# Pooled attention and a routed expert layer on one core: the order of VectorE's routing operations, a tile for softmax factors, one start-up multiplication and the last rows

## The chip, the core and the metric

The kernel runs on one core of one Trainium2 chip. A core has TensorE (PE; its weight loads are a row of their own, PEld), VectorE (DVE), ScalarE (ACT), GpSimd (POOL) and SyncE (SP), which issues transfers here. The engines run their own instruction streams in order and wait for one another by semaphores. The metric is device time of one execution in microseconds (us); lower is better.

## The reference, cut to what matters

All arrays are float32: q, k, v are 8 batches x 8 heads x 576 positions x 64. Keys and values are averaged over 8 neighbouring positions (72 pooled keys). The attention output, reordered to 4608 tokens x 512, goes to a layer of 8 experts, of which each token uses the one with the largest logit.

```python
k_p = k.reshape(B, H, 72, 8, D).mean(axis=3)
v_p = v.reshape(B, H, 72, 8, D).mean(axis=3)
scores = (q @ k_p.T) / sqrt(D)
scores = scores - scores.max(-1)
attn = exp(scores); attn = attn / (attn.sum(-1) + 1e-9)
x = attn @ v_p                      # to 4608 tokens x 512
logits = x @ w_gate + modality_bias[modality_id]
e_idx = argmax(logits, axis=1)
probs = softmax(logits)             # with + 1e-9 in the sum
gate_w = probs[arange(N), e_idx]
for e in range(8):
    mask = e_idx == e
    h = maximum(x[mask] @ w1[e], 0)         # 512 x 1024
    out[mask] = gate_w[mask, None] * (h @ w2[e])   # 1024 x 512
```

## The kernel before

The attention phase (about the first 185 us) works through 36 tiles of 128 query positions in 20 steps. Two batches make five steps: two of two tiles, one *mixed* step with a single tile made of the last 64 positions of both batches, and two more of two tiles. A loop over n pipelines the steps in software: in one pass it transposes the probabilities of step n-1, multiplies them with the values, and makes the scores of steps n+1 and n+2.

Of each half step w the scores (`s_pe`, TensorE, L548 in mixed steps, L554 in others) go to `s_dve`: VectorE takes row maxima `mx` (L561) and subtracts them to `sb` (L564); `s_act` takes the exponentials `pe` (L576, L577). `t_pe` transposes them (`pp`, L583; the tail by `t4_pe`, L595) and ScalarE copies them to `pt` (L588, L602). `a_pe` multiplies `pt` with the value operand `vw` (L618, L622) into `av`. The value operand holds for each head 64 pooled values, 8 columns of values already multiplied by the gate matrix, so that logits come out of the same product, and one column of ones, so that the softmax sum does too. `v_operand` (L388 to L400) builds it out of pooled values `vp` with two masks `m_a`, `m_b` that keep one of two heads; `v_gate` (L411 to L418) computes the gate columns with TensorE in a corner of a score bank, `spare[1]`, and ScalarE copies them out (L414, L415, L417).

`x_dve` then turns `av` into the output: `s8`, the eight sums (L641, `r`), their reciprocals (L643), the logits of the eight heads `lg` (L645), and the output row times the factor, `xb` (L651, two instructions). A *late* tile, the second tile of a step from the third group on, is not divided here: ScalarE copies the raw output `xo` (L648) and the eight factors stand in extra columns of `xb`, where the expert phase applies them; their reciprocal is written there directly. `xb` goes to the table `xs` in memory (L658, L661).

Routing works on groups of nine tiles (two batches). `route(g)` returns a list of small operations: the sum over heads (L700), the addition of the bias (L701), the maximum (L702), the subtraction and ScalarE's exponential `ex` (L705, L706), the choice of expert (L709 to L711), the sum of exponentials (L728 to L730), the gate value and its four stores to `xs` (L733, L736, L738), counts (L741) and the ranks within an expert. They don't run at once: they go on a list `drip`, and `gap(n)`, called between VectorE's other operations, issues the next n of it. `gap` is called in `s_dve` between maxima and subtraction, in `x_dve` behind the sums, behind the reciprocal and at its end, and twice in the loop. So the program's order on each engine is written out by these calls. Group 0 begins to drip in step 6, group 1 in step 11, group 2 in step 16; the last group's list is run behind the loop.

GpSimd meanwhile averages keys and values (L303 to L305), builds `bias_all` (L473 to L478), and adds some masks.

The expert phase (about 185 to 617 us) handles slots of 256 rows that one expert gets: rows are gathered and transposed, `hidden(f)` makes one of eight 128-wide blocks of the hidden layer (L170, with ScalarE and VectorE splitting the result into `hx` parts, L172, L174), `second(f)` multiplies it with w2 (L1186). Each runs as three matmul groups of split operands. `evac` scales a slot's rows by the gate value (L1162). The last slot ends in `end` or, when at most 128 rows of it are in use, in `end_half`, as in the run profiled here: blocks `hidden(f)` and `second(f - 1)` alternate, then `last_rows` scales the rows, one half by VectorE (L1261) and one by ScalarE (L1262), and a scatter (L1329) writes them.

## Time and profile before

| What | us |
|---|---|
| Three runs | 621.42, 624.14, 624.22 |
| Median of the three | 624.14 |
| The profiled execution | 624.82 |
| Its span, first to last instruction | 623.1 |
| TensorE busy | 604.3 (97%) |
| VectorE busy | 420.0 (67%) |
| ScalarE busy | 347.5 (56%) |
| GpSimd busy | 258.8 (42%) |
| Mean granted clock of TensorE | 0.996 of full |

Busy times are averages over a phase of attention, in which all engines hand work to one another, and a phase of experts, in which TensorE is never idle. A place in the attention phase is therefore read from the timeline: a line there gives the start, the duration, the engine, the kernel's line, the operation, the tiles written and read, and in square brackets how long the engine had been idle before and whose work ended that. The granted clock says at which share of 2.4 GHz TensorE was let run: 0.50 is its lower level, 1.2 GHz. A time ahead of the bracket is the instruction's own, so an instruction that is held while it runs shows as a longer duration and not as idle time.

### The profile page before, as it was taken

The numbers are of one execution on the slowest core, as the hardware profiler recorded it, in microseconds if no ns is written. First come the engines' busy times: TensorE is split into PE (matmuls) and PEld (weight loads), VectorE is DVE, ScalarE is ACT, GpSimd is POOL, SyncE is SP. The second block draws the span as 40 slices with busy tenths as digits, with TensorE's granted clock in tenths as the row PEclk, the third lists the DMA queues.
The fourth block names the chain that finished last, engine by engine and source line by source line (L and its number), as shares of the span: only waits on it lengthen the run. The fifth ranks groups of instructions, "written<-read, shape, count | busy, mean of one in ns | idle before, by whom it ended". The sixth has DMA issues, their size and how long they took to land.

```text
span 623.1 us, 12548 instructions
## 1 busy us (share of the span) xinstructions
PE 604.3 (97%) x4281; PEld 548.5 (88%) x4281; DVE 420.0 (67%) x803; ACT 347.5 (56%) x657; POOL 258.8 (42%) x326
## 2 busy tenths in 40 slices
PE   6899999999999999999999999999999999999996
PEld 5789889888898998999999999999999999999995
DVE  5857798789958578566666666666666665665661
ACT  3666576788541455555555555555555555555551
POOL 7789968663000451432532532522523522522510
PEclk9999899999999999999999999999999999999999
DMA  9999979874213710210210362210215510210200
GB/s 257 301 293 325 353 201 372 259 245 137 58 45 87 263 53 35 70 36 34 70 36 35 129 210 70 69 36 35 69 36 173 192 44 22 70 37 35 69 32 25
DMA packets 61178, 76.59 MB, mean 123 GB/s; under 512 B 15407, under 2 KB 39983, under 8 KB 61104
## 3 DMA queue, kind: packets, MB, share of 16 engines
q1 hardware_dynamic: 55104, 55.98, 28.9%
q0 software_dynamic: 6000, 19.72, 9.7%
q8 instruction: 36, 0.59, 0.4%
q14 instruction: 38, 0.31, 0.2%
HBM read 119.40 MB, written 19.45 MB: 223 GB/s over the span
## 4 chain that ended last, share of the span: by engine, by line
PE 79%; DVE 5%; issue 4%; POOL 4%; DMA 3%; ACT 2%; SPq 1%; POOLq 0%; ACTq 0%; DVEq 0%
PE op L1186 31%; PE hp L170 30%; PE av L618 4%; PE xt L161 2%; PE sc L554 2%; PE av L622 2%; DMA v<-in_v_dram 1%; PE pp L583 1%; PE ph L170 1%; PE pq L529 1%; DMA out_dram<-ob,sidx 1%; POOL v L303 1%; DVE sb L564 1%; DVE hl L139 1%; DVE mx L561 1%
## 5 line engine op out<-in xcount | busy, mean ns | idle before, releaser
L136 ACT CAST hl<-raw 128x1024 fp32r<-128x1024 f32 x138 | 144.8, 1049 | 138.6 <-PE op L1186 136.6
L170 PE MATMUL hp<-xh,hl 128*128 128x256 f32 x1152 | 186.1, 284 | 0.0
L139 DVE TENSOR_TENSOR hl<-raw,hl 128x1024 fp32r<-128x1024 f32 x144 | 183.7, 1277 | 0.0
L170 PEld LDWEIGHTS hp<-xh,hl 128*128 128x128 f32 x1152 | 166.1, 189 | 10.5
L1186 PE MATMUL op<-hl,hh 128*128 128x512 f32 x554 | 173.5, 394 | 0.0
L143 POOL DMA_INDIRECT xg<-xs,gidx x38 | 55.7, 1465 | 222.9 <-DVE ob L1162 158.0
L174 DVE SCALAR_TENSOR_TENSOR hlo<-hp,hh 128x256 fp32r<-128x256 f32 x139 | 58.8, 423 | 127.4 <-ACT hh L172 127.4
L1186 PE MATMUL op<-hl,hlo 128*128 128x512 f32 x277 | 108.4, 391 | 0.0
L1186 PEld LDWEIGHTS op<-hl,hh 128*128 128x128 f32 x554 | 94.8, 189 | 12.1
L170 PE MATMUL hp<-xl,hl 128*128 128x256 f32 x576 | 92.0, 282 | 0.0
L172 ACT ACTIVATE hh<-hp 128x256 fp32r<-128x256 f32 x139 | 53.4, 384 | 49.2 <-PE hp L170 44.9
L1168 POOL DMA_INDIRECT out_dram<-ob,sidx x36 | 52.3, 1453 | 66.6 <-DMA out_dram<-ob,sidx 37.0
L170 PEld LDWEIGHTS hp<-xl,hl 128*128 128x128 f32 x576 | 79.0, 190 | 0.0
L1186 PEld LDWEIGHTS op<-hl,hlo 128*128 128x128 f32 x277 | 52.0, 188 | 11.8
L618 PE MATMUL av<-vw,pt 128*128 128x146 f32 (+1 forms) x320 | 50.8, 298 | 2.2 <-ACT pt L588 1.1
L152 POOL TENSOR_TENSOR xg<-xg 128x512 f32<-128x512 f32 x34 | 41.1, 1212 | 25.1 <-DMA xg<-xs,gidx 25.0
L618 PEld LDWEIGHTS av<-vw,pt 128*128 128x128 f32 (+1 forms) x320 | 40.7, 183 | 4.7 <-ACT pt L588 2.2
L554 PE MATMUL sc<-kt,qt 128*128 128x144 f32 x256 | 37.3, 289 | 0.6 <-ACT qt L535 0.5
L164 DVE TENSOR_TENSOR xl<-xt,xh 128x512 fp32r<-128x512 f32 x38 | 24.5, 685 | 15.6 <-ACT xh L163 15.6
L554 PEld LDWEIGHTS sc<-kt,qt 128*128 128x128 f32 x256 | 33.2, 190 | 1.5 <-ACT qt L535 0.9
L561 DVE TENSOR_REDUCE mx<-sc 128x8 f32<-128x576 f32 (+1 forms) x40 | 27.7, 692 | 9.3 <-PE sc L554 7.2
L622 PE MATMUL av<-vw,pt 128*128 128x146 f32 (+1 forms) x160 | 31.4, 295 | 0.7 <-POOL vw L418 0.4
(236 smaller groups left out, 721.2 us busy)
## 6 DMA issues: line engine op xcount, KB each, us to landing
raw<-in_moe_w_dram SPq DMA_DIRECT2D x304, 256.0 KB
xs<-xb SPq DMA_DIRECT2D x16, 528.0 KB
k<-in_k_dram SPq DMA_DIRECT2D x7, 1024.0 KB
v<-in_v_dram SPq DMA_DIRECT2D x7, 1024.0 KB
q<-in_q_dram SPq DMA_DIRECT2D x7, 1024.0 KB
v<-in_v_dram SPq DMA_DIRECT2D x16, 128.0 KB
xs<-xb SPq DMA_DIRECT2D x8, 132.0 KB
k<-in_k_dram SPq DMA_DIRECT2D x4, 256.0 KB
```

Source lines behind the costliest of these rows:

```text
L136: nc.scalar.copy(hl[f][:, 0, :], raw[f])
L139: eng.tensor_sub(hl[f][:, 1, :], raw[f], hl[f][:, 0, :].bitcast(F32))
L143: nc.gpsimd.indirect_dma_start(out=xgs[(2 * s + tt) % len(xgs)], out_offset=None, in_=xs[0:rows, :], in_offset=IndirectOffsetOnAxis(idx[:, ...
L152: nc.gpsimd.tensor_tensor(xv, xv, x[:, RX:RX + H].rearrange("p (h o) -> p h o", o=1).to_broadcast([P, H, HD]), op=ALU.mult)
L170: nc.tensor.matmul(ph, hl[f][:, w, d * P:(d + 1) * P], x[:, d, :], start=(n == 0 and d == 0), stop=(n == 2 and d == ND - 1))
L172: nc.scalar.activation(hh, ph, AF.Relu)
L174: nc.vector.scalar_tensor_tensor(hlo, ph, 0.0, hh.bitcast(F32), op0=ALU.max, op1=ALU.subtract)
L554: nc.tensor.matmul(dst, qt[:, i, :], kt[b % NB][:, :, h * SPL:(h + 1) * SPL], start=True, stop=True)
L618: nc.tensor.matmul(av[hs, u, 2 * VC * gg:2 * VC * (gg + 1)], pt[:, c, hs], vw[y][:, c].rearrange("p a x -> p (a x)"), start=(gg == 0), sto ...
L622: nc.tensor.matmul(dst4[hs], pt4[:, hs], v4[y][:, 2 * u:2 * u + 2, :], start=False, stop=True)
L1168: nc.gpsimd.indirect_dma_start(out=out[:, :], out_offset=IndirectOffsetOnAxis(idx.bitcast(U32), 0), in_=ob, in_offset=None, bounds_check=N ...
L1186: nc.tensor.matmul(o[tt], l[:, ts_], hl[f][:, w, D:2 * D], start=(f == 0 and n == 0), stop=(f == NF - 1 and n == 2))
```

## The change

Five edits:

- `gap` gets an argument `long`. The first two operations of each group's list, the sum over heads and the bias addition, are kept in a set `long_ops` and are issued only by calls with `long` set: those at the end of `x_dve`, the two behind it in the loop and the one that empties the list after the loop.
- `s_dve` no longer calls `gap` in mixed steps.
- The reciprocals go to a tile `ri` of their own (four buffers). For late tiles ScalarE copies the eight of them into the columns of `xb`.
- For batch 0 the second masked copy of the values (`m_b`) is made by VectorE in place of ScalarE.
- In `end_half` the last `hidden` block stands right behind the one before it, and the last three `second` products follow. `last_rows` is one VectorE operation.

```diff
             nc.scalar.activation(dw[:, :, 0, 0:HD], vp, AF.Copy, scale=m_a)
-            nc.scalar.activation(dw[:, :, 1, 0:HD], vp, AF.Copy, scale=m_b)
+            if b:
+                nc.scalar.activation(dw[:, :, 1, 0:HD], vp, AF.Copy, scale=m_b)
+            else:
+                nc.vector.tensor_scalar_mul(dw[:, :, 1, 0:HD], vp, m_b)
...
-        def gap(n=2):
+        long_ops = set()
+
+        def gap(n=2, long=False):
             for _ in range(n):
-                if drip and drip[0] not in held:
+                if drip and drip[0] not in held and (long or drip[0] not in long_ops):
                     drip.pop(0)()
...
             nc.vector.reduce_max(mx, scv, axis=AX.X)
-            gap()
+            if jj is not None:
+                gap()
...
-            r = xw[:, z, RX:RX + H].rearrange("p (u h) -> p u h", u=2) if late else s8
+            r = ap.tile([P, 2, 4], F32, tag="ri", bufs=4, name=f"ri_{t}")
...
                 nc.scalar.copy(xo.rearrange("p (u h d) -> p u h d", u=2, h=4), avv[:, :, :, 0:HD])
+                nc.scalar.copy(xw[:, z, RX:RX + H].rearrange("p (u h) -> p u h", u=2), r)
...
-            gap(2)
+            gap(2, True)
...
             add(lambda: V.tensor_add(lg, lg, bias_all[:, sl, :]))
+            long_ops.update(ops)
...
-            gt = xg[2 * s % 4][:, D:D + 1]
-            nc.vector.tensor_scalar_mul(obl[:, 0:D // 2], o[0][:, 0:D // 2], gt)
-            nc.scalar.activation(obl[:, D // 2:D], o[0][:, D // 2:D], AF.Copy, scale=gt)
+            nc.vector.tensor_scalar_mul(obl, o[0], xg[2 * s % 4][:, D:D + 1])
...
-            for f in range(f0, NF):
+            for f in range(f0, NF - 1):
                 hidden(f, at[f])
-                second(f - 1, (0,), at[f - 1])
-            second(NF - 1, (0,), at[NF - 1])
+                if f < NF - 2:
+                    second(f - 1, (0,), at[f - 1])
+            hidden(NF - 1, at[NF - 1])
+            for f in range(NF - 3, NF):
+                second(f, (0,), at[f])
```

What stands in a row on VectorE in step 6, where group 0 begins (`lgr` are the group's summed logits, `m` their maximum; a name's number tells apart its uses), before:

```order
L561 TENSOR_REDUCE mx_1_1064<-sc_1_1038 128x8
L700 TENSOR_REDUCE lgr_1014<-lg_497 128x72
L701 TENSOR_TENSOR lgr_1014<-lgr_1014,bias_all 128x72
L564 TENSOR_TENSOR sb_1_1068<-sc_1_1038,mx_1_1064 128x576
L641 TENSOR_SCALAR r_1082<-av_1057 128x8
L702 TENSOR_REDUCE m_0_1016<-lgr_1014 128x9
L643 RECIPROCAL r_1082<-r_1082 128x8
L705 TENSOR_TENSOR lgr_1014<-lgr_1014,m_0_1016 128x72
L645 TENSOR_TENSOR lg_1081<-av_1057,r_1082 128x64
L651 TENSOR_TENSOR xb_172<-av_1057,r_1082 128x256 x2
```

and with the change (lines are those of the changed kernel, some 9 further on):

```order
L566 TENSOR_REDUCE mx_1_1073<-sc_1_1047 128x8
L571 TENSOR_TENSOR sb_1_1075<-sc_1_1047,mx_1_1073 128x576
L648 TENSOR_SCALAR r_1089<-av_1066 128x8
L650 RECIPROCAL ri_1090<-r_1089 128x8
L652 TENSOR_TENSOR lg_1088<-av_1066,ri_1090 128x64
L659 TENSOR_TENSOR xb_172<-av_1066,ri_1090 128x256 x2
L708 TENSOR_REDUCE lgr_1023<-lg_497 128x72
L709 TENSOR_TENSOR lgr_1023<-lgr_1023,bias_all 128x72
L711 TENSOR_REDUCE m_0_1025<-lgr_1023 128x9
L714 TENSOR_TENSOR lgr_1023<-lgr_1023,m_0_1025 128x72
L566 TENSOR_REDUCE mx_0_1116<-sc_0_1104 128x2x2
```

The four routing operations stood between the step's maxima, subtraction and factors; they now stand behind `xb`, ahead of the next step's maxima.

On ScalarE in step 16, where group 2 begins (`vg_7` and the two operations ahead of it are the last batch's gate columns, `hl` a weight block, `xb_175<-av` the raw output of a late tile), before:

```order
L535 COPY qt_0_2314<-pq_0_2315 128x512
L706 ACTIVATE ex_2199<-lgr_2198 128x72
L414 ACTIVATE vw_138<-sc_1_2219,m_a 128x4x8
L415 ACTIVATE vw_138<-sc_1_2219,m_b 128x4x8
L417 COPY vg_7_2333<-sc_1_2219 128x32
L851 CAST hl_2256<-raw_1878 128x512
L648 COPY xb_175<-av_2337 128x512
L588 COPY pt_2363<-pp_2358 128x512
```

and with the change:

```order
L539 COPY qt_0_2346<-pq_0_2347 128x512
L417 ACTIVATE vw_138<-sc_1_2250,m_a 128x4x8
L418 ACTIVATE vw_138<-sc_1_2250,m_b 128x4x8
L420 COPY vg_7_2362<-sc_1_2250 128x32
L860 CAST hl_2287<-raw_1902 128x512
L715 ACTIVATE ex_2230<-lgr_2229 128x72
L655 COPY xb_175<-av_2366 128x512
L656 COPY xb_175<-ri_2374 128x8
L595 COPY pt_2395<-pp_2390 128x512
```

The exponential of the logits moved from before the gate columns to behind the weight block, and a copy of `ri` stands behind that of the raw output, ahead of the copy to `pt`. In steps 6 and 11 the exponential keeps its place on ScalarE, ahead of the exponentials of the second half of the scores and of the gate columns.

On TensorE at the end of `end_half` (`hp` is a hidden block out of weight block `hl`, `op` the second product of `hx`), before:

```order
L170 MATMUL hp0_2821<-xh0_84,hl6_2383 128x256 x4
L170 MATMUL hp0_2821<-xl0_85,hl6_2383 128x256 x4
L170 MATMUL hp0_2821<-xh0_84,hl6_2383 128x256 x4
L1186 MATMUL op0_0_2817<-hl5_2256,hx2_0_2856 128x512 x2
L1186 MATMUL op0_0_2817<-hl5_2256,hx2_1_2857 128x512
L170 MATMUL hp1_2822<-xh0_84,hl7_2596 128x256 x4
L170 MATMUL hp1_2822<-xl0_85,hl7_2596 128x256 x4
L170 MATMUL hp1_2822<-xh0_84,hl7_2596 128x256 x4
L1186 MATMUL op0_0_2817<-hl6_2383,hx3_0_2858 128x512 x2
L1186 MATMUL op0_0_2817<-hl6_2383,hx3_1_2859 128x512
L1186 MATMUL op0_0_2817<-hl7_2596,hx4_0_2860 128x512 x2
L1186 MATMUL op0_0_2817<-hl7_2596,hx4_1_2861 128x512
```

and with the change:

```order
L170 MATMUL hp0_2865<-xh0_84,hl6_2415 128x256 x4
L170 MATMUL hp0_2865<-xl0_85,hl6_2415 128x256 x4
L170 MATMUL hp0_2865<-xh0_84,hl6_2415 128x256 x4
L170 MATMUL hp1_2866<-xh0_84,hl7_2634 128x256 x4
L170 MATMUL hp1_2866<-xl0_85,hl7_2634 128x256 x4
L170 MATMUL hp1_2866<-xh0_84,hl7_2634 128x256 x4
L1195 MATMUL op0_0_2861<-hl5_2287,hx2_0_2900 128x512 x2
L1195 MATMUL op0_0_2861<-hl5_2287,hx2_1_2901 128x512
L1195 MATMUL op0_0_2861<-hl6_2415,hx3_0_2902 128x512 x2
L1195 MATMUL op0_0_2861<-hl6_2415,hx3_1_2903 128x512
L1195 MATMUL op0_0_2861<-hl7_2634,hx4_0_2904 128x512 x2
L1195 MATMUL op0_0_2861<-hl7_2634,hx4_1_2905 128x512
```

The product with `hl5` moved from between the last two hidden blocks to behind them.

## Rows read from the trace of the kernel before

**Rows 1.** Page, part 1: each engine's busy us (share of span) and instructions.

```profile
...
PE 604.3 (97%) x4281; PEld 548.5 (88%) x4281; DVE 420.0 (67%) x803; ACT 347.5 (56%) x657; POOL 258.8 (42%) x326
...
```

**Rows 2.** Busy time by stretch: length, PE, PEld, DVE, ACT, POOL, PEclk, DMA share, GB/s.

```profile
...
69.00:72.00 3.00, 3.00 (x13) 2.99 (x14) 2.29 (x8) 1.09 (x6) 2.69 (x7) 0.50 1.05 345
...
113.00:150.00 37.00, 35.93 (x311) 32.26 (x311) 30.23 (x89) 30.83 (x79) 20.47 (x33) 1.00 0.61 197
...
150.00:170.00 20.00, 19.31 (x173) 17.51 (x173) 19.02 (x55) 12.72 (x35) 2.02 (x3) 1.00 0.39 109
...
200.00:600.00 400.00, 400.00 (x2652) 364.11 (x2651) 258.51 (x355) 218.71 (x322) 142.06 (x102) 1.00 0.24 77
...
```

**Rows 3.** Timeline 59.5 to 67.5 us (start, duration, engine), then line L701's group.

```profile
...
63.42 1.19 DVE L700 TENSOR_REDUCE lgr<-lg 128x72 f32<-128x576 f32 x1
...
64.23 0.41 PE L622 MATMUL av<-vw,pt 128*128 128x146 f32 x2
...
65.24 1.27 POOL L303 TENSOR_TENSOR k<-k 128x512 f32<-128x512 f32 x1
65.32 1.29 DVE L701 TENSOR_TENSOR lgr<-lgr,bias_all 128x72 f32<-128x72 f32 x1 [0.70 <-POOL bias_all L478]
...
L701 DVE TENSOR_TENSOR lgr<-lgr,bias_all x4: 234/234/1286, 65.3 to 188.0; 128x72 f32<-128x72 f32 x4
...
```

**Rows 4.** The same timeline, 65.5 to 74.5 us.

```profile
...
67.33 0.63 PE L411 MATMUL sc<-wgb,vt 128*128 128x32 f32 x4 [0.58 <-DVE sb L564]
...
67.97 0.26 ACT L706 ACTIVATE ex<-lgr 128x72 f32<-128x72 f32 x1 [2.21 <-DVE lgr L705]
67.99 0.74 DVE L651 TENSOR_TENSOR xb<-av,r 128x256 f32<-128x256 f32 x2
...
68.79 1.34 PE L618 MATMUL av<-vw,pt 128*128 128x146 f32 x4 [0.49 <-DVE xb L651]
...
69.90 0.19 ACT L417 COPY vg<-sc 128x32 f32<-128x32 f32 x1
...
72.46 0.44 PEld L548 LDWEIGHTS sc<-kt,qt 128*64 128x64 f32 x8 [0.17 <-issue]
...
```

**Rows 5.** Timeline 104 to 114.5 us, the same place one group later.

```profile
...
105.19 0.41 PE L622 MATMUL av<-vw,pt 128*128 128x146 f32 x2
...
106.78 0.70 DVE L705 TENSOR_TENSOR lgr<-lgr,m 128x72 f32<-128x72 f32 x1
...
107.51 0.26 ACT L706 ACTIVATE ex<-lgr 128x72 f32<-128x72 f32 x1 [0.79 <-DVE lgr L705]
...
110.47 0.44 PEld L548 LDWEIGHTS sc<-kt,qt 128*64 128x64 f32 x8 [0.17 <-issue]
...
111.16 0.21 DVE L645 TENSOR_TENSOR lg<-av,xb 128x64 f32<-128x64 f32 x1
...
111.45 0.59 ACT L648 COPY xb<-av 128x512 f32<-128x512 f32 x1 [1.82 <-PE sc L595]
...
112.58 0.77 PE L618 MATMUL av<-vw,pt 128*128 128x146 f32 x4 [0.71 <-ACT pt L588]
...
```

**Rows 6.** Timeline 149 to 152 us, VectorE.

```profile
...
149.66 0.23 DVE L705 TENSOR_TENSOR lgr<-lgr,m 128x72 f32<-128x72 f32 x1
...
150.90 0.17 DVE L641 TENSOR_SCALAR r<-av 128x8 f32<-128x8 f32 x1 [0.63 <-PE av L622]
...
```

**Rows 7.** Timeline 17 to 20 us, VectorE.

```profile
...
19.25 0.76 DVE L561 TENSOR_REDUCE mx<-sc 128x8 f32<-128x576 f32 x1 [0.80 <-PE sc L554]
...
```

**Rows 8.** Timeline 612 to 623.1 us, then line L1162's group.

```profile
...
616.08 1.60 PE L1186 MATMUL op<-hl,hx 128*128 128x512 f32 x6
...
617.17 0.19 PEld L1186 LDWEIGHTS op<-hl,hx 128*128 128x128 f32 x1 [0.16 <-DVE hx L174]
...
618.23 0.47 ACT L1262 ACTIVATE obl<-op,xg 128x256 f32<-128x256 f32 x1 [1.57 <-DVE obl L1261]
...
L1162 DVE TENSOR_SCALAR ob<-op,xg x18: 740/742/751, 200.5 to 600.1; 128x512 f32<-128x512 f32 x18
...
```

More of the change, by code (lines that the diff above doesn't have):

```diff
@@ L558, in s_dve @@
             nh = 2 * len(steps[n][2])
+            jj = steps[n][1]
             scv = scs.pop((n, w))[:, :, 0:nh * SPL].rearrange("p u (h s) -> p u h s", s=SPL)
@@ L975 @@
                 x_dve(old[0])
-            gap(2)
+            gap(2, True)
             if nxt and n:
@@ L999 @@
                 x_dve(old[1])
-            gap(2)
+            gap(2, True)
             if n != N - 1:
@@ L1005 @@
             release()
-            gap()
+            gap(2, True)
         loads(N + 1)
```

## The prediction

> **What bounds the kernel now.** I read the page's busy times first, then busy time by stretch, then the timelines of the places that the change touches. TensorE is busy for 604.3 of the 623.1 us of the span [rows 1], and from 200 to 600 us for 400.00 of 400.00 at full clock [rows 2]: the expert phase is TensorE's and nothing in this change shortens its matmuls. All idle time of TensorE together is 623.1 - 604.3 = 18.8 us, much of it while the first data arrive and after the last matmul, so a reordering has only a few us to win, in the attention phase and at the very end. The profiled execution took 624.82 us for a span of 623.1, so 1.7 lie around the span; it stands 0.7 above the median of the three runs, 624.14.
>
> **Long routing operations, group 0 (step 6).** Here the kernel pays for them. VectorE has finished the row maxima and could subtract at once; instead it runs L700 (1.19 us at 63.42), waits 0.70 for GpSimd's bias_all, then runs L701 for 1.29, where its usual time is 0.234 (the group's median) [rows 3]. So sb comes more than 2 us late, and TensorE stands 0.58 before the gate product L411 (released by sb) and 0.49 before the product L618 (released by xb) [rows 4]. Behind those gaps the granted clock in 69 to 72 us is 0.50, the level of 1.2 GHz, with TensorE busy all 3.00 us [rows 2]: matmuls that would need 1.5 us at full clock, so 1.5 more. What there is to win is 0.58 + 0.49 + 1.5 = 2.6 us.
>
> The order with the change: maxima, sb, the three small operations on factors, xb, and only then reduction, bias, maximum and subtraction. TensorE's product ends at 64.23 + 0.41 = 64.64 [rows 3]; three factor operations (0.17 for one of them [rows 6], 0.6 for the three with issue) and the pair xb, 0.74 [rows 4], end at 66.0. The reduction takes 1.2 and three operations follow, 0.25 each with issue: the logits are there at about 68.0 to 68.2. ScalarE's ex keeps its place in ScalarE's queue: it waits for these logits, ran at 67.97 before [rows 4], and runs at about 68.25. Queued behind it there are qt, the exponentials, and the gate copies up to vg at L417, which ended 69.90 + 0.19 - 67.97 = 2.12 behind the start of ex [rows 4]: now at 70.4. The score matmuls L548 write the bank that L417 reads. They began at 72.46 [rows 4] and, with the two waits and the half clock gone, can begin at 70.4: **a gain of 2.0**. If all of it comes back it is 2.6. The low end is 0.5: the bias addition and the subtraction find GpSimd busy (2.69 of 3.00 us here [rows 2]) and both take what they took at worst, 1.29 for 0.23 [rows 3] and 0.70 for 0.23 [rows 5], together 1.5 more. I take 2.0 because the median of the bias addition is 0.234 [rows 3] and only one of four met such a neighbour.
>
> The slow L701 ran from 65.32 to 66.61, and GpSimd's addition L303 from 65.24 to 66.51 [rows 3]: the two end within 0.1 us. The Trainium skill ("SBUF — State Buffer", Who interferes with whom) states that a VectorE instruction with two SBUF inputs and a GpSimd instruction that reads SBUF exclude each other for a whole instruction; this row agrees. By that page the moved additions and subtractions would meet GpSimd again as often as it is busy, which is the second rival's case below.
>
> **The same, group 1 (step 11).** Here no stall answers to the long operations: L701 is short, TensorE waits for none of them, and moving them only makes ex late. The product ends at 105.60 [rows 5], xb 1.35 later at 106.95, the reduction at 108.15, the subtraction at 108.9 (109.4 with the 0.70 of [rows 5]). So ex moves from 107.51 to between 108.95 and 109.4. With the same 2.12 to vg's end, that moves from 109.63 to between 111.1 and 111.5, and L548, which began at 110.47, 0.84 behind it [rows 5], begins 0.6 to 1.0 later. Part of this is absorbed: TensorE waited 0.71 before L618 at 112.58 for pt, which stands behind the copy xo at 111.45 [rows 5]. Two more matmul groups stand between L548 and L618, and with them L618 comes 0.05 to 0.5 later: **a cost of 0.3** (0 to 0.8, the high end without the absorption).
>
> **The same, group 2 (steps 16 and 17).** In 150 to 170 us VectorE is the fullest engine but TensorE: 19.02 of 20.00 us [rows 2]. Before, maximum and subtraction of the logits (0.23 for the subtraction) ran where VectorE next waited 0.63 for TensorE at 150.90 [rows 6], so they cost nothing. Mixed steps no longer take them between maxima and subtraction, and they come behind that wait, in busy time: 0.45 later, so **a cost of 0.4** (0 to 0.9; 0 if the earlier sb gives it back to TensorE, 0.9 if the reduction too falls there).
>
> **Queues that the steps are moved past.** The four stores of the gate columns per group follow their reciprocal and now stand on SyncE's queue behind some loads of q, k and v for group 0, and behind a pair of raw weight loads for group 1. The loads come earlier, and nothing reads the gates before the gathers, which follow long after: 0. GpSimd's and, but for the end, TensorE's order are the same.
>
> **Factors in their own tile.** The eight tiles left undivided (second of a step, group 2 on) get one more ScalarE copy of 128x8. The nearest row is vg's copy, 0.19 us [rows 4]. In return xo's copy might start before the factors are ready; but it still waits for the same tile's VectorE product (lg at 111.16, ending 0.08 before the copy's start [rows 5]), so I count no gain. Eight copies are 1.5 us of ScalarE; on the path copy, pt, L618, as at 112.58, lie about three: **a cost of 0.4** (0 to 0.8, half of them).
>
> **First masked values by VectorE.** At the start TensorE and the loads set the time, and VectorE waits 0.80 for the scores at 19.25 [rows 7]; one multiplication of 128x256 moved to it, half the pair xb or 0.4 [rows 4], is hidden there, and costs that much if the cover fails. **0** (0 to 0.4).
>
> **The end.** The last six matmuls run from 616.08 to 617.68, and the last weight load among them waits 0.16 for the second part of hx [rows 8], which TensorE's last hidden block has only just made possible. With that block ahead of the last three second products, six matmuls instead of three lie between it and the product that needs its hx, and this wait goes: -0.15. The scaling of the rows ended at 618.23 + 0.47 = 618.70, 1.02 behind the matmuls, since ScalarE's half waited for VectorE's; one operation of 128x512 takes 0.742 in the group of 18 [rows 8], with 0.04 to start: -0.24. **-0.4** together (-0.3 to -0.5).
>
> **Sum.** -2.0 + 0.3 + 0.4 + 0 + 0.4 + 0 - 0.4 = -1.3. The profiled execution of 624.82 would become 623.5; against the median, 624.14 - 1.3 = **622.8**.
>
> **The rivals.**
> (a) Everything is won: step 6 gives 2.6, groups 1 and 2 and the copies cost 0.3 in all, the end gives 0.4: -2.7, so 621.4. For it: the costs sit where other waits may absorb them. Against it: L548 in step 6 still has ScalarE's queue ahead of it.
> (b) The wait comes back elsewhere: the moved addition and subtraction meet GpSimd as L701 did, ex holds ScalarE's queue, and step 6 gives only 0.5, step 11 costs 0.8: -0.5 + 0.8 + 0.4 + 0.4 - 0.4 = +0.7, so 624.8. For it: GpSimd's share in that stretch. Against it: three of four L701 at the median.
> (c) Slower: ex, late by 1.5 to 1.9 in step 11, holds qt, the exponentials and vg, TensorE stands twice (about 0.4 before the transposes, 0.6 before L548), and its clock falls to half for 3 us as it did in 69 to 72 behind gaps of 0.58 and 0.49 [rows 2, 4]; the same kind of gap keeps step 6 at half clock. Step 11 then costs 0.8 + 1.5 = 2.3 and step 6 gives 2.0 - 1.5 = 0.5: -0.5 + 2.3 + 0.4 + 0.4 - 0.4 = +2.2, so 626.3. It decides if ex runs later than about 109.2 in step 11, where L548 is held for 0.8. Against it: behind TensorE's wait of 0.71 at 112.58 [rows 5] the clock of the stretch from 113 us stayed at 1.00 [rows 2]. The Trainium skill ("TensorE: Matmul & The Clock Gate", Part 1) calls the low clock the default state that activity lifts, so that a gap's price is not its length alone; the 0.50 of 69 to 72 agrees.
> That the change does not do what it says can be left out for the order of VectorE, where it shows; for the factors' tile it is part of that term.
>
> **How the numbers follow.** Forecast 0.5, (a) 0.2, (b) 0.2, (c) 0.1. Times of one kernel spread over 2.8 us (621.42 to 624.22), so each case stands for about 1.4 to either side. The range goes from (a)'s 621.4 less 1.4, 620.0, to (b)'s 624.8 with 1.4, 626.2; what it leaves out is most of (c) and the edges. A difference under 0.5%, 3.1 us, cannot be told from none: faster is below 621.0, slower above 627.3. Faster: a tenth of the forecast, 0.05, and four tenths of (a), 0.08: 0.13. Slower: three tenths of (c), 0.03, and a tenth of (b), 0.02: 0.05. Same: 0.82.
>
> **What would show it.** Right: in the stretch of step 6 TensorE's two waits are gone, the clock is 1.00 and L548 begins near 70.4; ex in step 11 near 109.0; L701's successor takes 0.23; VectorE ends the kernel with one 0.74. Wrong: half clock left in step 6, or a new one near 110 us, or a pt that comes later by more than 0.2 in each undivided tile. The sum fails most easily at step 6, which carries it, if the low clock there has another cause than these two waits.

## The result and the profile after

| | Before | After |
|---|---|---|
| Median of 12 runs, us | 623.43 (621.42 to 625.92) | 625.22 (623.34 to 627.8) |
| The profiled execution's span, us | 623.1 | 626.1 |
| Ratio after / before | | 1.0036, 95% interval 1.002 to 1.0051 |

A second comparison on another occasion (e5_after, below) gave 1.0022, 1.0004 to 1.004. The changed kernel is slower by 0.2 to 0.4%, 1.4 to 2.2 us; the forecast was 1.3 us faster. The time lies inside the range given, on the other side of no change, and within the 0.5% that were called same. Both profiled executions of the changed kernel, this one (627.8) and that of e5_after (629.41), are the longest of their twelve, so what they show need not be what a usual execution does.

The page's first lines after, to be read beside [rows 1]: the busy time of TensorE, VectorE and ScalarE is what it was within 0.3 us, so the 3.0 us of span are waits: 0.4 of them before step 6, 2.3 in the stretches of the table below and 0.2 behind them.

```profile
span 626.1 us, 12557 instructions
...
PE 604.2 (96%) x4281; PEld 547.5 (87%) x4281; DVE 420.3 (67%) x804; ACT 347.6 (56%) x663; POOL 255.5 (41%) x326
...
```

The same stretches as in [rows 2] (length, PE, PEld, DVE, ACT, POOL, granted clock, DMA share, GB/s):

```profile
...
69.00:72.00 3.00, 3.00 (x14) 2.98 (x14) 0.34 (x1) 1.57 (x6) 2.69 (x6) 0.55 1.05 340
...
113.00:150.00 37.00, 35.52 (x308) 31.34 (x306) 29.47 (x88) 30.86 (x83) 21.71 (x35) 1.00 0.54 172
150.00:170.00 20.00, 19.16 (x171) 17.16 (x168) 18.48 (x55) 12.81 (x36) 3.69 (x5) 1.00 0.40 118
200.00:600.00 400.00, 400.00 (x2651) 364.07 (x2651) 259.01 (x365) 217.98 (x321) 138.92 (x102) 1.00 0.24 77
...
```

In the expert phase TensorE is busy all 400 us as before. The half clock behind step 6 is still there (0.55 in 69 to 72). What changed in step 6 is the reason, in the timeline that answers to [rows 3, 4]:

```profile
...
67.65 0.23 DVE L709 TENSOR_TENSOR lgr<-lgr,bias_all 128x72 f32<-128x72 f32 x1
...
67.75 0.63 PE L533 MATMUL pq<-ident,q 128*128 128x128 f32 x4 [1.15 <-DMA q<-in_q_dram]
...
68.22 0.53 PE L414 MATMUL sc<-wgb,vt 128*128 128x32 f32 x4
...
68.45 0.26 ACT L715 ACTIVATE ex<-lgr 128x72 f32<-128x72 f32 x1 [2.25 <-DVE lgr L714]
...
69.01 1.08 PE L625 MATMUL av<-vw,pt 128*128 128x146 f32 x4
...
70.38 0.19 ACT L420 COPY vg<-sc 128x32 f32<-128x32 f32 x1
...
72.81 0.71 PE L552 MATMUL sc<-kt,qt 128*64 128x144 f32 x8
...
```

The chain is as forecast: the bias addition takes 0.23, TensorE no longer waits for sb (L414) nor for xb (L625), ex starts at 68.45 and vg ends at 70.57, in a profile that ran 0.45 us later up to here. But TensorE now waits 1.15 us one product sooner, at L533, for a load of q. The gap only changed its cause; the clock fell behind it as before. That product stands ahead of both products whose waits are gone, so it isn't a wait that they had hidden: its load (the first of the two in these lines) was issued at 55.2 us in place of 53.4, before any moved operation. First the line of before, then that of after:

```profile
...
L242 SPq DMA_DIRECT2D q<-in_q_dram x2: 368/570/771, 53.4 to 66.5; - x2
...
L242 SPq DMA_DIRECT2D q<-in_q_dram x2: 368/368/368, 55.2 to 68.2; - x2
...
```

Further on, in steps 7 to 8, stands a wait that no row of before had:

```profile
...
73.88 1.26 POOL L303 TENSOR_TENSOR v<-v 128x512 f32<-128x512 f32 x1
...
73.98 1.19 DVE L738 TENSOR_SCALAR sm<-sm 128x9 f32<-128x9 f32 x1
...
76.44 1.27 POOL L303 TENSOR_TENSOR v<-v 128x512 f32<-128x512 f32 x1
76.50 1.22 DVE L750 TENSOR_TENSOR cum<-cum,dc 128x8 bf16<-128x8 bf16 x1
...
77.65 0.21 DVE L652 TENSOR_TENSOR lg<-av,ri 128x64 f32<-128x64 f32 x1
...
77.79 0.74 DVE L659 TENSOR_TENSOR xb<-av,ri 128x256 f32<-128x256 f32 x2
...
78.67 0.74 PE L625 MATMUL av<-vw,pt 128*128 128x146 f32 x4 [1.10 <-DVE xb L659]
...
```

The small operations of the list have moved back too, because the list is strictly in order. cum, 128 x 8 elements, now stands between a tile's factors and takes 1.22 us, from 76.50 to 77.72, the end of GpSimd's addition at 76.44 + 1.27 = 77.71. Before, it ran at 72.43, where TensorE waited for nothing that it held up:

```profile
...
72.43 0.83 DVE L741 TENSOR_TENSOR cum<-cum,dc 128x8 bf16<-128x8 bf16 x1
...
```

After, it stands in TensorE's way. The addition of 1e-9 (L738), 0.17 in other groups, takes 1.19 beside another such addition. TensorE waits 1.10 for xb.

It need not be cum. In e5_after, the second profile of the same kernel, TensorE waits 1.04 at this place, but cum takes only 0.42; there the expert's choice `oh` is the one that ends with a GpSimd addition:

```profile
...
73.64 1.42 DVE L720 TENSOR_TENSOR oh<-w,m 128x72 bf16<-128x72 f32 x1
...
73.70 1.26 POOL L303 TENSOR_TENSOR v<-v 128x512 f32<-128x512 f32 x1
...
```

In group 1, against [rows 5]:

```profile
...
109.22 0.84 DVE L709 TENSOR_TENSOR lgr<-lgr,bias_all 128x72 f32<-128x72 f32 x1
...
110.63 0.26 ACT L715 ACTIVATE ex<-lgr 128x72 f32<-128x72 f32 x1 [2.80 <-DVE lgr L714]
...
112.57 0.19 ACT L420 COPY vg<-sc 128x32 f32<-128x32 f32 x1
...
112.81 0.71 PE L552 MATMUL sc<-kt,qt 128*64 128x144 f32 x8 [0.64 <-ACT vg L420]
...
114.06 0.66 PE L625 MATMUL av<-vw,pt 128*128 128x146 f32 x4
...
116.08 0.84 DVE L750 TENSOR_TENSOR cum<-cum,dc 128x8 bf16<-128x8 bf16 x1
...
117.86 0.74 PE L625 MATMUL av<-vw,pt 128*128 128x146 f32 x4 [0.28 <-DVE xb L659]
...
```

As worked out, ex is late and L552 waits for vg, and L625 comes later: from the same earlier matmul to here it is 0.19 us more. Here the bias addition met GpSimd (0.84; in e1, e6, e7 and e13 too, 0.81 to 0.84). In step 12 cum does it again (0.84) and TensorE waits 0.28 for xb. The group of the four cum:

```profile
...
L750 DVE TENSOR_TENSOR cum<-cum,dc x4: 106/498/1224, 76.5 to 193.0; 128x8 bf16<-128x8 bf16 x4
...
```

One undivided tile, and the group of the new copies (count, shortest, median, longest in ns):

```profile
...
120.37 0.59 ACT L655 COPY xb<-av 128x512 f32<-128x512 f32 x1 [1.60 <-PE pp L590]
...
120.85 0.20 ACT L656 COPY xb<-ri 128x8 f32<-128x8 f32 x1
...
120.95 0.59 ACT L595 COPY pt<-pp 128x512 f32<-128x512 f32 x1
...
```

```profile
...
L656 ACT COPY xb<-ri x8: 200/200/237, 113.1 to 188.5; 128x8 f32<-128x8 f32 x8
...
```

The copy of 0.20 stands between the raw output and pt, and pt starts 0.58 behind the raw output's copy, where the same pair in the kernel before (118.55 and 119.03) is 0.48 apart: 0.1 a copy. And the end, against [rows 8]:

```profile
...
618.20 2.25 PE L1195 MATMUL op<-hl,hx 128*128 128x512 f32 x9
...
620.49 0.75 DVE L1269 TENSOR_SCALAR obl<-op,xg 128x512 f32<-128x512 f32 x1 [1.25 <-PE op L1195]
...
```

Nine matmuls without a gap, then one operation: the rows are scaled 0.79 us behind the matmuls' end at 620.45, in place of 1.02. The execution's end didn't follow. The last scatter took longer to land: us from its issue to its landing in the profiles of before, after and e5_after:

```profile
...
out_dram<-obl,sl POOLq DMA_INDIRECT x1, 2.6
...
out_dram<-obl,sl POOLq DMA_INDIRECT x1, 3.1
...
out_dram<-obl,sl POOLq DMA_INDIRECT x1, 4.8
...
```

So from the last matmul's end to the end of the span it is 5.42 us before, 5.63 after and 7.32 in e5_after. In the six profiles with the old end this landing takes 2.6 to 2.8; in the eleven with the new end 2.6 to 2.7 in five, 3.1 in four and 4.8 in two (e5_after, e15_mended). On the two chips that are known to have profiles of both ends it is 2.6 to 2.8 for either, so the chip is as likely a cause as the edit; no run here separates them.

### The profile page after: what moved, and what is told of

Same layout as the page of the kernel before. It is cut to its first block, busy times and chain, and to the rows that moved or that the text cites. A ratio compares the mean times of both kernels' runs of the same rounds, so it can differ in the third digit from the quotient of the medians.

```text
span 626.1 us, 12557 instructions
## 1 busy us (share of the span) xinstructions
PE 604.2 (96%) x4281; PEld 547.5 (87%) x4281; DVE 420.3 (67%) x804; ACT 347.6 (56%) x663; POOL 255.5 (41%) x326
## 4 chain that ended last, share of the span: by engine, by line
PE 78%; DVE 7%; DMA 6%; issue 4%; ACT 2%; SPq 1%; POOL 0%; POOLq 0%; DVEq 0%; ACTq 0%
PE op L1195 31%; PE hp L170 30%; PE av L625 4%; PE xt L161 2%; PE sc L558 2%; DMA q<-in_q_dram 2%; PE av L629 2%; DMA v<-in_v_dram 2%; PE ph L170 1%; PE pp L590 1%; DMA out_dram<-ob,sidx 1%; PE pq L533 1%; DMA qm<-in_q_dram 1%; DVE xb L659 1%; DVE mx L566 1%
## 5 line engine op out<-in xcount | busy, mean ns | idle before, releaser
L172 ACT ACTIVATE hh<-hp 128x256 fp32r<-128x256 f32 x139 | 53.4, 384 | 49.1 <-PE hp L170 44.8
L1177 POOL DMA_INDIRECT out_dram<-ob,sidx x36 | 49.7, 1381 | 64.6 <-DMA out_dram<-ob,sidx 38.2
L625 PE MATMUL av<-vw,pt 128*128 128x146 f32 (+1 forms) x320 | 50.6, 297 | 2.4 <-DVE xb L659 1.6
L625 PEld LDWEIGHTS av<-vw,pt 128*128 128x128 f32 (+1 forms) x320 | 40.4, 182 | 5.2 <-ACT pt L595 1.8
L595 ACT COPY pt<-pp 128x512 f32<-128x512 f32 x36 | 21.2, 588 | 19.2 <-PE pp L590 18.7
```

Of the source, the lines that this page charges most:

```text
L172: nc.scalar.activation(hh, ph, AF.Relu)
L625: nc.tensor.matmul(av[hs, u, 2 * VC * gg:2 * VC * (gg + 1)], pt[:, c, hs], vw[y][:, c].rearrange("p a x -> p (a x)"), start=(gg == 0), sto ...
L1177: nc.gpsimd.indirect_dma_start(out=out[:, :], out_offset=IndirectOffsetOnAxis(idx.bitcast(U32), 0), in_=ob, in_offset=None, bounds_check=N ...
```

## Where the time went, place by place

Up to the end TensorE runs the same matmuls in the same order in all these kernels, so the time from the start of its n-th matmul to that of a later one can be taken from each trace. The table gives these distances in us: the stretch of step 6 (65.88 to 74.21 in the profile before), steps 7 to 8 (to 80.64), 8 to 10 (to 109.44), 11 (to 113.38), 12 (to 120.83), 13 to 15 (to 145.90), 16 and 17 with what follows (to 169.56). "Half clock" tells whether TensorE ran a part of step 6 at half clock. The labels are those of the experiments.

| Kernel | Step 6 | 7-8 | 8-10 | 11 | 12 | 13-15 | 16-17 | Half clock |
|---|---|---|---|---|---|---|---|---|
| before | 8.33 | 6.43 | 28.80 | 3.94 | 7.45 | 25.07 | 23.67 | yes |
| e3_end (same order) | 7.89 | 6.36 | 28.79 | 3.94 | 7.45 | 25.04 | 23.67 | yes |
| e4_mb (same order) | 7.73 | 6.36 | 28.80 | 3.92 | 7.45 | 25.07 | 23.67 | yes |
| e2_ri (same but copies) | 6.58 | 6.43 | 28.79 | 4.04 | 7.57 | 25.16 | 23.77 | no |
| e12_ri_vec (same but copies) | 6.81 | 6.44 | 28.79 | 3.93 | 7.45 | 25.05 | 23.74 | no |
| after | 7.73 | 7.70 | 28.80 | 4.13 | 8.09 | 25.43 | 24.10 | yes |
| e5_after | 7.75 | 7.69 | 28.81 | 4.13 | 8.08 | 25.47 | 24.11 | yes |
| e6_after_no_ri | 5.58 | 6.36 | 28.80 | 4.11 | 7.95 | 25.07 | 24.13 | no |
| e1_long | 6.15 | 6.63 | 29.09 | 4.12 | 7.95 | 25.08 | 24.13 | no |
| e7_after_cum | 5.80 | 6.36 | 29.20 | 4.11 | 7.58 | 25.44 | 24.41 | no |
| e13_q_first | 5.70 | 6.66 | 29.12 | 4.13 | 8.08 | 25.17 | 24.13 | no |
| e15_mended | 5.72 | 6.65 | 29.09 | 4.12 | 7.96 | 25.05 | 24.19 | no |
| e8_best1 | 6.15 | 6.36 | 29.17 | 3.93 | 7.45 | 25.06 | 23.66 | no |
| e14_best1_q | 5.57 | 6.36 | 29.91 | 3.96 | 7.45 | 25.08 | 23.67 | no |
| e10_best2 | 4.88 | 6.36 | 30.15 | 4.86 | 8.29 | 25.07 | 23.67 | no |
| e9_bias4 | 5.83 | 6.43 | 28.79 | 3.93 | 7.45 | 25.04 | 23.67 | no |
| e11_best3 | 5.85 | 6.43 | 28.80 | 3.95 | 7.45 | 25.08 | 23.67 | no |

From step 11 on the same order gives the same distance within 0.1 us, so small costs can be read there (one exception: e13 has the order of after, and 25.17 for its 25.43 in steps 13 to 15). Steps 6 to 10 hang on when loads arrive and differ from run to run. What lies ahead of the table, 64.1 to 66.5 us but for e9 and e11, differs most; what lies behind it is the same within 0.1 us up to the end.

## The experiments

Theory P: the costs stand where the table shows them. Against it stood the prediction's own terms (P0), a late start through the masked copy (D), and the load of q as the one thing that ends step 6 (L).

### The four parts alone

The order of the routing operations alone (the edits to `gap`, its calls and `s_dve` of the change):

```diff
-                if drip and drip[0] not in held:
+                if drip and drip[0] not in held and (long or drip[0] not in long_ops):
...
-            gap()
+            if steps[n][1] is not None:
+                gap()
```

> Only the two edits to the order of the routing operations (long ones behind xb, none between maxima and subtraction in mixed steps); factors, start and end as before. Theory P, read from the two traces by where each TensorE instruction falls behind: step 6 gives 0.6 of the 2.0 forecast, because TensorE then waits for the load of q and keeps its half clock; in steps 7 and 8 a small addition, cum, is pushed into the next tile's factors, meets GpSimd and costs 1.2; step 11 costs 0.3 and cum in step 12 another 0.4: +1.3, ratio about 1.002. The prediction's terms instead: -2.0 + 0.3 + 0.4 = -1.3, ratio 0.998. In P's profile TensorE's product in step 8 waits about 1 us for xb.

Ratio 1.0003, 0.9988 to 1.0019: not the 0.998 of P0, and P's 1.002 lies at the edge of the interval. In this profile TensorE waited for no load, and the clock stayed up (stretches as above, then TensorE's waits from 60 to 82 us: total, times, longest):

```profile
...
67.00:70.00 3.00, 2.60 (x18) 2.01 (x17) 2.83 (x10) 1.85 (x7) 2.77 (x6) 1.00 1.07 352
...
```

```profile
...
PE sc L549 <- ACT vg L417: 0.6, 1, 0.6
```

Step 6 took 6.15 in place of 8.33, and 0.6 of it is the wait for vg that the prediction had. The costs stood in later steps: +0.2 in 7 to 8, where P had named a wait of 1 us, +0.3 in 8 to 10, +0.2 in 11, +0.5 in 12, +0.46 in 16 and 17.

The factors' tile alone:

```diff
-            r = xw[:, z, RX:RX + H].rearrange("p (u h) -> p u h", u=2) if late else s8
+            r = ap.tile([P, 2, 4], F32, tag="ri", bufs=4, name=f"ri_{t}")
...
+                nc.scalar.copy(xw[:, z, RX:RX + H].rearrange("p (u h) -> p u h", u=2), r)
```

> Only the factors' own tile with its extra ScalarE copy in eight undivided tiles. Theory P: five of the eight copies lie on ScalarE's way to pt and cost TensorE 0.2 each: +1.0, ratio 1.0016. The prediction's term: +0.4, ratio 1.0006. A rival, that the copies are hidden: 0.

Ratio 1.0019, 1.0002 to 1.0036. By places it costs 0.1 in each of four stretches, 0.4 together. This kernel has the old order in step 6, and TensorE waited there (the same two views):

```profile
...
67.00:70.00 3.00, 3.00 (x29) 2.63 (x28) 2.93 (x14) 2.02 (x9) 2.69 (x7) 1.00 1.05 321
69.00:72.00 3.00, 2.58 (x23) 2.17 (x23) 2.36 (x10) 2.01 (x6) 2.84 (x7) 1.00 1.02 391
...
```

```profile
...
PE av L618 <- DVE xb L652: 0.9, 2, 0.5
...
```

Yet the clock stayed at 1.00. In e12_ri_vec (below) the same two waits as in the kernel before, 0.53 for sb and 0.50 for xb, left it at 1.00 too (the second wait for xb lies at the end of the step):

```profile
...
PE av L618 <- DVE xb L652: 0.9, 2, 0.5
PE sc L411 <- DVE sb L564: 0.5, 1, 0.5
```

With two waits of 0.2 to 0.6 us each in step 6 the clock fell in three of five profiles of the old order, and in the changed kernel's two behind the one of over 1 us; in the eight others of the new order, with waits of 0 to 1.0 us in all, it didn't.

The end alone, and the masked copy alone:

```diff
-            nc.vector.tensor_scalar_mul(obl[:, 0:D // 2], o[0][:, 0:D // 2], gt)
-            nc.scalar.activation(obl[:, D // 2:D], o[0][:, D // 2:D], AF.Copy, scale=gt)
+            nc.vector.tensor_scalar_mul(obl, o[0], xg[2 * s % 4][:, D:D + 1])
```

> Only the end: the last hidden block ahead of the last three second products, and one VectorE operation for the rows. Both theories: -0.3 to -0.4, ratio 0.9995; the span's last scatter comes 1.3 us behind the last second product's end and not 1.3 + 0.3.

Ratio 0.9993, 0.9978 to 1.0009, in keeping with -0.3 but not told from nothing.

```diff
-            nc.scalar.activation(dw[:, :, 1, 0:HD], vp, AF.Copy, scale=m_b)
+            if b:
+                nc.scalar.activation(dw[:, :, 1, 0:HD], vp, AF.Copy, scale=m_b)
+            else:
+                nc.vector.tensor_scalar_mul(dw[:, :, 1, 0:HD], vp, m_b)
```

> Only the masked copy of batch 0 by VectorE. Theory P: hidden, 0. Rival D: it delays the start, where the changed kernel's TensorE stood 0.9 us later at 13.5 us and 0.45 later at 41 us: +0.5 to +0.9, ratio about 1.001.

Ratio 0.9992, 0.9978 to 1.0006. Rival D is not borne out: the upper end of the interval is +0.4 us, under D's +0.5. The profiles alone would not settle it: the start, to the matmul at 41 us, differs by 1.6 us among the six that don't have this edit, and the 0.45 that the changed kernel showed there lies inside that.

### The changed kernel and what is taken out of it

> The changed kernel again, beside its variants on one chip. If the four parts add up (+0.03 + 0.19 - 0.07 - 0.08% measured apart), ratio 1.0007; if they don't, the first measurement's 1.0036 comes again. By place, its TensorE should fall behind in steps 7 and 8 for xb and cum (0.2 to 1.2, by where GpSimd's additions happen to lie), 0.3 in step 11, 0.4 in step 12, and 0.2 at each of four or five undivided tiles.

Ratio 1.0022, 1.0004 to 1.004; its profile repeats the first within 0.05 us in every stretch of the table, the wait for q's load included, but the wait in steps 7 to 8 has another operation behind it (oh, above), and the last scatter landed 1.7 us later. The four parts apart add to 1.0007; the whole measured slower than its parts, but the intervals allow the difference to be nothing.

Without the factors' tile (the edit of e2_ri undone in the changed kernel):

```diff
-            r = ap.tile([P, 2, 4], F32, tag="ri", bufs=4, name=f"ri_{t}")
+            r = xw[:, z, RX:RX + H].rearrange("p (u h) -> p u h", u=2) if late else s8
...
-                nc.scalar.copy(xw[:, z, RX:RX + H].rearrange("p (u h) -> p u h", u=2), r)
```

> The changed kernel with the late tiles' reciprocals written into the columns of xb as before, so without the eight ScalarE copies. If the copies cost what they cost alone (0.19%), it is 1.0 to 1.2 us under the changed kernel on this chip; if the tile is not what costs, the same time.

Ratio 1.0005, 0.999 to 1.0019: 1.1 us under the changed kernel by the two ratios (0.8 by the medians), about as much as the tile cost alone. The places give less: 0.1 in step 12 and 0.4 in 13 to 15. In its profile TensorE waited neither for q nor, in steps 7 to 8, for xb, though its order is that of the changed kernel there: both are a matter of the moment.

The copies by VectorE in the kernel before:

```diff
-                nc.scalar.copy(xw[:, z, RX:RX + H].rearrange("p (u h) -> p u h", u=2), r)
+                nc.vector.tensor_copy(xw[:, z, RX:RX + H].rearrange("p (u h) -> p u h", u=2), r)
```

> The factors' own tile alone, as in the run of that part, but the eight copies into the columns of xb by VectorE instead of ScalarE. If the cost (0.19% alone, 0.17% taken out of the changed kernel) is ScalarE's copy ahead of pt, it is gone: ratio 1.000 to 1.0005. If the tile or the wait for it costs, 1.0015 to 1.002 again.

Ratio 1.0002, 0.9988 to 1.0016, and every stretch from step 11 on is that of before but the last (+0.07). The group of the copies:

```profile
...
L649 DVE COPY xb<-ri x8: 155/166/640, 108.8 to 182.5; 128x8 f32<-128x8 f32 x8
...
```

So by place the cost is ScalarE's copy ahead of pt and not the tile; the two ratios' intervals overlap. Its size is less sure (e15_mended, below).

The small operations behind xb:

```diff
             add(lambda: V.tensor_scalar_add(sm, sm, 1e-9))
+            long_ops.add(ops[-1])
...
             add(lambda: V.tensor_add(cum[:, g + 1, :], cum[:, g, :], dc))
+            long_ops.add(ops[-1])
```

> The changed kernel with two more operations of each group kept out of the tile's factors: the addition of 1e-9 to the sums and cum are issued only behind xb, as the long ones are. If cum's meeting GpSimd between the factors costs TensorE 1.2 in step 8 and 0.4 in step 12, those waits for xb are gone and the time falls by up to 1.6; if the long operations' place is what costs, no change.

Ratio 1.002, 1.0004 to 1.0036: no gain to be measured. The places named are mended (6.36 in 7 to 8, 7.58 in 12; but e6 has 6.36 without this edit), and yet 0.4 comes back in 8 to 10, where TensorE waits 0.9 for sb in place of 0.5, and 0.3 in 16 and 17. That cum among the factors costs 0.5 in step 12 is shown. In steps 7 to 8 the moved operations cost 1.3 in both profiles of the changed kernel, which is not cum's alone (it took 0.42 in e5); that they cost this in most runs is not shown.

### What ends step 6

bias_all one step earlier, all orders but GpSimd's untouched:

```diff
-        at(hook_0, 5, modality_terms)
+        at(hook_0, 4, modality_terms)
```

> The kernel before with one edit of another kind: GpSimd builds bias_all one step earlier (step 4 in place of 5), the order of all other engines untouched. It takes away only what L701 waits for in step 6. If the late bias is what holds the softmax chain there, VectorE's wait of 0.70 and with it most of TensorE's 0.58 and 0.49 are gone without any cost in steps 8 to 17: -0.7 to -2.4 (the larger if the clock stays at 1.00 behind it), ratio 0.996 to 0.999. If the load of q ends last in step 6 anyway, no change, and TensorE waits there for that load.

Ratio 1.0012, 0.9991 to 1.0033. Step 6 took 5.83 without any change of order, which fits the late bias having held the chain. It does not show it: TensorE came to the step 2.6 us later (68.50), the bias addition was done at 63.76, and everything else had that time too. For the stretch ahead took 28.2 in place of 24.6:

```profile
...
PE pv L396 <- POOL vp L305: 1.4, 1, 1.4
...
PE pv L395 <- POOL vp L305: 0.5, 1, 0.5
...
```

GpSimd's operations stand back to back before step 6: what it does earlier for the bias it does later for the pooled values, TensorE waits for those, and the half clock falls there, at 64 us.

The load of q ahead of the load of k in the changed kernel:

```diff
-                         (3, load_k4, 4), (3, load_k, 5), (4, load_q, 3), (4, load_v4, 4),
+                         (3, load_k4, 4), (4, load_q, 3), (4, load_k, 5), (4, load_v4, 4),
```

> The changed kernel with one load order turned round on SyncE's queue: the load of q that step 6 needs is issued ahead of a 1 MB load of k that is needed three steps later. Theory L: the changed kernel's step 6 ends on that load of q (TensorE waited 1.1 and 1.2 us for it in both profiles), so the gain of the order is lost there, the clock still falls, and cum then meets GpSimd: with the load first, TensorE's wait is gone, from start to start the stretch of step 6 is 5.5 in place of 7.7 us, and the time falls by 1.2 to 3: ratio 0.998 to 1.000. Rival: the loads before 66 us are bound by the transfers' rate as a whole, another load is late instead, and the ratio stays at 1.002 to 1.004.

Ratio 1.002, 1.0003 to 1.0037. In the profile the wait for q is gone and the clock of step 6 stays up, as theory L said, though e1 and e6 had no such wait without this edit. The largest waits left are those for vg in steps 6 and 11, and for sb (waits of TensorE, 30 to 130 us: total, times, longest):

```profile
...
PE sc L602 <- DVE sb L571: 1.3, 2, 0.8
PE sc L552 <- ACT vg L420: 1.3, 2, 0.6
...
```

Step 6 took 5.70 and all the gain was there; the time was not. L explains the profile, not the measurement.

The same with the copies by VectorE:

```diff
-                nc.scalar.copy(xw[:, z, RX:RX + H].rearrange("p (u h) -> p u h", u=2), r)
+                nc.vector.tensor_copy(xw[:, z, RX:RX + H].rearrange("p (u h) -> p u h", u=2), r)
```

> The changed kernel with both suspected losses mended: the eight copies of factors by VectorE, and the load of q ahead of that of k. If the copies cost 1.1 and the late q 1.2 to 3, the ratio is 0.997 to 0.999, under the one without this mend of the copies by 0.0015 or so; if only the copies count, 1.0005 as in the run without the factors' tile.

Ratio 1.002, 1.0006 to 1.0033: with q first, the copies' mend brought nothing. Of three pairs that differ in the copies two differ by 0.17% and this one by 0.00, 0.7 us on the mean; the places say 0.4 to 0.5 in the first two pairs and 0.2 in this one.

### Candidates

The new end, the masked copy, and the order changed for group 0 only, with cum and the addition to the sums behind xb:

```diff
+            if g == 0:
+                long_ops.update(ops)
```

> A candidate: the kernel before with the new end, the masked copy by VectorE, and the long operations behind xb for group 0 alone, with cum and the addition to the sums there too; groups 1 and 2 and the undivided tiles as before. From the parts: -1.0 for the two waits of step 6, -0.4 for the end, no cost in steps 8, 11, 12 and in group 2: ratio 0.998. If the load of q takes the place of the waits in step 6, only the end is left: 0.9993.

Ratio 0.9995, 0.9978 to 1.0011. With q's load first:

> The first candidate (new end, masked copy by VectorE, long operations of group 0 alone behind xb with cum and the addition to the sums) with the same load order. Theory L: its remaining wait for q, 0.3 in the profile, is gone: 0 to -1.0 against the candidate's 0.9995, ratio 0.998 to 0.9995. Rival: another load is late, 0.9995 or above.

Ratio 0.9991, 0.9974 to 1.0008. Groups 0 and 1 with all operations up to cum behind xb, and ex issued later:

```diff
+            def pick():
+                if g < EARLY_GROUPS:
+                    nc.scalar.activation(ex, lg, AF.Exp)
+                V.scalar_tensor_tensor(lg, lg, 0.0, per_t(w8, n), op0=ALU.is_equal, op1=ALU.mult)
+            add(pick)
```

> A candidate: new end, masked copy by VectorE, and for groups 0 and 1 every routing operation up to cum only behind xb, with ex issued on ScalarE behind the gate columns; group 2 and the undivided tiles as before. If the costs of the long operations' move are cum and the others among the factors and ex ahead of the gate columns, TensorE has no wait for xb in step 8, none for vg in steps 6 and 11, and steps 11 and 12 take what they took before (3.94 and 7.45 us by TensorE's starts): ratio 0.997 to 0.999. If it is the same as the kernel before, the gain of step 6 is not there outside the profile.

Ratio 0.9992, 0.9981 to 1.0003. Step 6 is the shortest of all, 4.88, 3.4 under the profile before and 1.8 under the old order at full clock, and steps 8 to 12 give back 3.1 (+1.35, +0.9, +0.8): rank operations that follow cum (arow, two of 128 x 128, 1.05) stand between maxima and subtraction there, and TensorE waits 1.67 for sb in step 8:

```profile
...
83.99 1.05 DVE L767 TENSOR_SCALAR arow<-iota_b,rkf 128x128 bf16<-128x128 bf16 x2
...
84.96 0.74 DVE L568 TENSOR_TENSOR sb<-sc,mx 128x576 f32<-128x576 f32 x1
...
85.85 0.30 PE L599 MATMUL sc<-ident,pe 128*128 128x128 f32 x1 [1.67 <-DVE sb L568]
...
```

> A candidate: the kernel before with the new end, the masked copy by VectorE and bias_all one step earlier. The sum of the three alone: -0.3, -0.3 and what the bias alone gives.

Ratio 1.0022, 1.0007 to 1.0036: the early bias is no gain here either. The three before it lie 0.27% to 0.45% under the changed kernel's two ratios, e8 beside it on the same chip; none can be told from the kernel before.

## Why the prediction was wrong

**Step 6, the term of -2.0, failed.** Its mechanism was seen: without the long operations TensorE's two waits go, and ex and vg come where the working put them (68.45 and 70.57 for 68.25 and 70.4, in a profile 0.45 later). Its size was wrong, because it took the half clock for a part of what the two waits cost. 1.5 of the 2.6 to be won was the half clock of one profile; the old order shows it in three profiles of five, the stretch being 7.7 to 8.3 with it and 6.6 to 6.8 without. And the new order doesn't rid step 6 of it: in two of five profiles (after and e5, of e1, e6 and e7 besides) TensorE waited over 1 us for a load of q, and the clock fell behind that. The prediction had marked this place as the weakest of its sum, if the low clock had another cause than the two waits. It named a new wait as a rival too, but on ScalarE's queue and on VectorE, not on a transfer. Like with like, the new order gains 0.9 where the clock stays up (5.8 on the mean of e1, e6, e7, e13 and e15, for 6.7 of e2 and e12), about the 1.07 of the two waits, and 0.2 where it falls (7.74 for 7.98). Over steps 6 to 8 the five profiles of the old order take 13.9 us on the mean (13.0 to 14.8), and after, e5, e6, e7 and e1 of the new one 13.5 (11.9 to 15.4): a gain of 0.3, not 2.0, in so few and so unlike profiles.

**The terms that were not there.** The list is in order, so holding its first operations back moves all behind them. The prediction followed two of them to their new places and ex with them, and not the rest. cum among the factors costs 0.5 in step 12 (e1 and e6: 7.95 for 7.45); the moved operations cost 0 to 1.3 in steps 7 to 8, by which of them is held beside GpSimd, and 0 to 0.3 in steps 8 to 10. Rival (b), the wait that comes back by meeting GpSimd, had the mechanism and 0.2 of the chance, and mostly the wrong instructions: in step 6 the bias addition was free (0.23), in step 11 it was held (0.84), and the dear meetings were those of cum, L738 and oh.

**Right or nearly so.** Step 11: 0.3 forecast, 0.18 measured by place, through vg as worked out. Group 2: 0.4 forecast, 0.46. The copies: 0.4 forecast, 0.2 to 0.5 by place; the runs put it at 0 to 1.1, so the term may be too small. The end: -0.4 forecast, -0.27 by place (1.02 to 0.79 for the rows, 0.04 for the matmuls; the 0.15 for a wait was too much, since the whole sequence gained only that 0.04); but that is up to the scaled rows, and the scatter's landing took it back in six of eleven profiles of the new end. The masked copy: 0 in both. Of rival (c) the half on step 11 did not happen: TensorE waited 0.64 there and its clock stayed. The half on step 6 did, in the changed kernel's two profiles, through the load.

**The sum with the measured terms:** -0.3 (steps 6 to 8) + 0.2 (8 to 10, of 0 to 0.3) + 0.2 (11) + 0.5 (12) + 0.45 (16 and 17) + 0.45 (copies, the upper of the two readings) - 0.3 (end, without the landing) = +1.2 us, where the two comparisons have 1.4 and 2.2 with 1 us to either side.

**Open.** e13 and e15 have neither the wait for q nor the half clock of step 6 in their profiles, their places are no more than 0.8 us above the old order without half clock (103.0 and 102.8 in all for 102.2 and 102.4), and their times are 1.2 us above. The profiles differ most where the table doesn't reach. At the end, e15's scatter takes 4.8 us to land, for 2.6 in the profile before, e13's 2.7. At the start, step 6 begins at 64.1 to 65.9 us in the five profiles of old order and start (before, e1, e2, e3, e12) and at 64.5 to 66.5 in the ten with the masked copy by VectorE (e9 and e11 apart): a spread as large as what is sought. Why q's load was issued late in the changed kernel's two profiles was not settled either. One explanation can be set aside: the mean granted clock, which is on record for every timed run, is no lower in the changed kernel (0.9976 over its 12 runs of e5's comparison, 0.9975 over the 35 of the kernel before on the same chip; 0.9984 in the first comparison), so it isn't slower by more time at half clock. Single profiles can't tell how often a run of either kernel waits in steps 6 to 8, nor whether the copies cost 0.2 or 1.1.

## What to carry to other kernels

Holding back the head of an ordered list moves everything behind it: follow each later operation to its new neighbours, above all the short ones that land in another chain. Before a stall is priced, look for the transfers due at the same place, and take the price of a clock drop only if several profiles show it. Where all engines hand work to one another, an operation that is moved out of one chain can be paid for in the next: four orders (e1, e8, e10, e14) shortened step 6 by 2.2 to 3.4 us against the profile before (0.5 to 1.8 against the old order at full clock), and none was measurably faster than the kernel before.

## What the runs showed of the hardware

A VectorE operation on 128 x 8 elements (cum) took 0.11 to 1.22 us in one kernel, the longest ending within 0.01 of a GpSimd addition that had begun just before it; and one with a single array as input (L738, 128 x 9) took 1.19, to 75.17, beside an addition that ended at 75.14. And the clock's fall in step 6 came and went between profiles of the same order: with waits of 0.58 and 0.49 us (before) it fell, with 0.53 and 0.50 (e12) it did not.
